# Rows of V as two half rows of 2080 bytes, and a scratch tensor with both batches side by side

## The chip, the core and the metric

The kernel runs on one core of one Trainium2 chip. The core has a matrix engine (TensorE, in the profile PE for the matmuls and PEld for its weight loads), a vector engine (DVE), a scalar engine (ACT), GpSimd (POOL) and a queue engine (SP) that here only starts transfers. Transfers between main memory (DRAM) and the on-chip memory (SBUF, 128 partitions) run on 16 DMA engines that all queues share. The metric is the device time of one execution in microseconds (us), lower is better.

## What is computed

A block-sparse attention, whose result goes through a token mixer. Cut to what matters:

```python
batch, n_heads, seq, head_dim = 4, 8, 768, 64     # 24 blocks of 32 tokens
mask = |blk_i - blk_j| <= 1, or blk_i or blk_j is 0 or 23
mask[block qb, block kb] = True for the 3 kb in sampled_blocks[qb]
attn = softmax(where(mask, q k^T / 8, -1e9));  x = attn @ v       # (4, 768, 512)

theta = x @ w_theta
y = einsum('ts,bsd->btd', w_tok_r, x * cos(theta)) + einsum(..., w_tok_i, x * sin(theta))
u = x + y
return u + maximum(u @ w_ch, 0)
```

## The kernel before

The attention works on two batches at a time (`bp` = 0, 1; in each the batches `b` = 0, 1, the pairs of head halves `e` = 0, 1). Within a pair of batches come first 8 wide units, which are the two outer blocks of queries against all keys, and then 22 ordinary units, one for each inner block `i` of 32 queries. An ordinary unit uses eight blocks of keys and values: three of the window, the three sampled ones, and the two outer ones. The work of one unit is spread over several rounds of one loop, `for n in range(len(units) + 2)`, so that different engines are on different units: scores (PE), row minimum (DVE), exponentials (ACT), transposes (PE, line 307), their copy (ACT, line 309), and the products with V (PE, line 318, `X`). The order on every engine is the order of this code; nothing is rearranged by a scheduler in the attention.

The values stand in DRAM as `vr`, one row of 1040 floats (4160 bytes) for each token and pair of batches: 2 batches x 2 x 4 heads x 65, where the 65th column is a one that makes the sum of the weights. Behind them stand 32 rows of zeros. Two tiles feed the products:

- `va` (two buffers) holds the window in partitions 0 to 95, block `k` in slot `k % 3`, and block 0 in partitions 96 to 127. Unit `i` loads two fresh blocks with `load_window` through SP: one transfer of 64 rows, or two of 32 where the slots wrap around. It is issued in the round before its use, when the unit two before has released the buffer.
- `vb` (`VB_BUFS = 3` buffers) holds the three sampled blocks in partitions 0 to 95 and block 23 in 96 to 127. `gather_v` fills it with one indirect transfer on POOL, whose row numbers stand in the table `rows`; blocks that are in the window or twice in the sample get rows of zeros. `Tables.make` works out `rows` once on DVE (lines 155 to 163).

`values` (PE) reads from both with `weigh`: 65 columns at offset `260 * (2 * b + e) + 65 * p`. `finish` scales the result and SP writes it to the scratch tensor in DRAM,

```python
xs = dram.tile([NP, 2, NB, P, P], F32, name="xs")      # pair, batch, block, row, column
```

which is two runs of 512 bytes for each of 128 rows of a unit. SP also carries the loads of `q` and of the raw weights (`raw_*`, decoded on the way by DVE and ACT); the ACT queue carries the next pair's keys (`kb`) and wide values (`vw`) once, at the change of pair. After the attention the token mix reads `xs` back (`load`, line 480, and `load_raw`, line 491), four blocks at a time in runs of 512 bytes, and is nearly all matmuls (lines 517 to 519, 555 to 557, 578 to 580).

Of the kernel before, what the change touches and what calls it, by code (L numbers as in the profile page):

```python
# [19 lines left out]
P = 128  # L20
NB = 24
NP = 2
ZEROS = float(768 * NP)
VB_BUFS = 3
# [92 lines left out]
class Tables:  # L117
# [6 lines left out]
    def make(self, nc, cp):  # L124
        raw = self.raw
        words = raw.rearrange("p (i k w) -> p i k w", k=3, w=2)
        given = cp.tile([P, 3, NB], F32, name="sb_given")
        nc.vector.tensor_copy(given, words[:, :, :, 0].rearrange("p i k -> p k i"))
        r = cp.tile([P, 3, NB], F32, name="sb_r")
        nc.vector.tensor_scalar(r, given, 0.0, float(NB - 1), op0=ALU.max, op1=ALU.min)  # L130
        self.block = cp.tile([1, NB * 3], I32, name="sb_block")
        nc.vector.tensor_copy(self.block.rearrange("p (i k) -> p k i", k=3), r[0:1])
        iota_i = cp.tile([P, NB], I32, name="iota_i")
        nc.gpsimd.iota(iota_i, pattern=[[1, NB]], base=0, channel_multiplier=0)
        qi = cp.tile([P, NB], F32, name="qi")
# [12 lines left out]
        nc.vector.scalar_tensor_tensor(t, r, float(NB - 1), r, op0=ALU.subtract, op1=ALU.mult)  # L148
        nc.vector.scalar_tensor_tensor(u, t, 0.0, u, op0=ALU.is_equal, op1=ALU.max)
        for k in range(1, 3):  # L150
            for j in range(k):
                nc.vector.tensor_tensor(t[:, j, :], r[:, k, :], r[:, j, :], op=ALU.is_equal)
                nc.vector.tensor_tensor(u[:, k, :], u[:, k, :], t[:, j, :], op=ALU.max)

        self.rows = rows = cp.tile([96, NP, NB], I32, name="rows")
        for k in range(3):
            g = slice(32 * k, 32 * k + 32)
            nc.vector.tensor_scalar(t[g, 0, :], u[g, k, :], -1.0, 1.0, op0=ALU.mult, op1=ALU.add)
            for bp in range(NP):
# [3 lines left out]
        nc.vector.tensor_scalar(rows, base, ZEROS, None, op0=ALU.add)  # L163


def attention(tc, qT, qE, kT, vr, sampled, xs, ident, pieces, follow):
# [8 lines left out]
    nc = tc.nc  # L175
    with ExitStack() as ctx, ExitStack() as early:
# [70 lines left out]
        def fresh(i, new):  # L247
# [6 lines left out]
                    runs.append([blk, 1])  # L254
            return runs

        def load_window(bp, i):
            va = vas[i % 2]
            if i <= 2:
                nc.sync.dma_start(va[96:128], vr[768 * bp : 768 * bp + 32])  # L260
            for b0, n in fresh(i, i <= 2):
                s0 = 32 * (b0 % 3)
                nc.sync.dma_start(va[s0 : s0 + 32 * n], vr[768 * bp + 32 * b0 : 768 * bp + 32 * (b0 + n)])
            st[bp, i]["va"] = va

        def gather_v(bp, i):
            vb = vbs[i % VB_BUFS]
            if i <= VB_BUFS:
                nc.sync.dma_start(vb[96:128], vr[768 * bp + 736 : 768 * bp + 768])
            nc.gpsimd.indirect_dma_start(  # L270
                out=vb[0:96],
                out_offset=None,
                in_=vr,
                in_offset=bass.IndirectOffsetOnAxis(ap=tab.rows[:, bp, i : i + 1], axis=0),
            )
            st[bp, i]["vb"] = vb

        def scores(bp, i):
# [52 lines left out]
        def values(bp, i):  # L331
            s = st[bp, i]
            s["X"] = x = ps_x.tile([P, 4, 65], F32, tag="X", name=f"X{bp}_{i}")
            for b in range(2):
                for e in range(2):
                    weigh(x, 2 * b + e, s["T"], 2 * e + b, s["va"], 96 if i == 1 else 128, 260 * (2 * b + e), True, False)
                    weigh(x, 2 * b + e, s["T"], 4 + 2 * e + b, s["vb"], 96 if i == NB - 2 else 128, 260 * (2 * b + e), False, True)
# [42 lines left out]
        def finish_wide(bp, b, e, z):  # L380
            if (e, z) == (1, 1):
                xo = normalised(f"{bp}_w{b}", xws[bp, b])
                nc.sync.dma_start(xs[bp, b, 0 : NB : NB - 1].rearrange("z r c -> r z c"), xo.rearrange("r (z e) d -> r z (e d)", z=2))
            if (b, z) == (0, 1):
                load_v_wide(bp, 1, e)

# [63 lines left out]
def token_mix(tc, w, ch_pieces, xs, outT, bias, nb):  # L450
# [8 lines left out]
    with ExitStack() as late, ExitStack() as ctx:  # L459
# [14 lines left out]
        def load(k):  # L474

            b, h, j = at(k)
            xa[k] = xp.tile([P, 4, 4, 32], F32, tag="xa", name=f"xa{k}")
            src = xs[b // 2, b % 2, 4 * j : 4 * j + 4].rearrange("i (p q) c -> p i q c", p=4)
            for p in range(4):
                nc.sync.dma_start(xa[k][:, p].rearrange("s c u -> s (c u)"), src[p])  # L480

        def load_raw(k, pool=None):
# [8 lines left out]
            nc.sync.dma_start(xr[b, j].rearrange("r i c u -> r i (c u)"), xs[b // 2, b % 2, 4 * j : 4 * j + 4].rearrange("i r c -> r i c"))  # L491

        def tok(b, j):
            return [t[:, :, 128 * (j % 3) : 128 * (j % 3) + 128] for t in xT[b, j // 3]]
# [141 lines left out]
def sparse_attention_then_token_mix(ctx, tc, qT, qE, kT, vr, sampled, w_theta, w_tok_r, w_tok_i, w_ch, outT):  # L636
# [78 lines left out]
```

## Time and profile before

| what | value |
|---|---|
| median of 3 runs | 638.6 us |
| lowest and highest run | 634.63 and 641.9 us |
| span of the profiled execution, first to last instruction | 635.0 us |
| PE, DVE, ACT, POOL busy | 563.2, 463.5, 361.0, 45.6 us |
| packets: SP queue q1, gathers q0, ACT queue q10 | 73088, 4928, 1856 |
| megabytes: q1, q0, q10 | 72.99, 17.57, 4.74 |
| share of 16 DMA engines: q1, q0, q10 | 39.2%, 10.7%, 2.1% |

Only the span is known of the profiled execution; its own device time was not recorded beside it. It stands 3.6 us below the median, inside the range of the three runs.

How to read the views. A row of a group has the line, engine and operation, what it writes and reads, its shape and count, then the busy time and the mean of one in ns, then the idle time of the engine just before and what ended it. The chain of waits goes back from the end to what released each step. A row of the DMA queues has the packets, the megabytes and the time that the packets took, as a share of 16 engines over the stretch; since packets can overlap a little, a share may pass 100%. A wait line reads: who waited, for whom, us in total, times, longest.

### The profile page before, as it was taken

Reading aid. Unit: us, or ns where it says so; the run is one execution under the profiler, and the core shown is the slowest. Engines: PE = TensorE matmul, PEld = TensorE weight load, DVE = VectorE, ACT = ScalarE, POOL = GpSimd, SP = SyncE. Lnnn points to the kernel's source line nnn. Section 1 sums busy time; section 2 is a strip of 40 time slices with the busy share of each in tenths; the row PEclk is TensorE's granted clock in tenths of the full one; section 3 lists DMA queues with packets and bytes.
Section 4 is the critical chain, followed back from the end, with each engine's and each line's share of the span. In section 5 each row is a group of like instructions: output and inputs, shape, how many; then the busy total and the mean of one; then the engine's idle time right before and its main releaser. Section 6 shows DMA issues by size and latency. Waiting matters only on the chain.

```text
span 635.0 us, 19148 instructions
## 1 busy us (share of the span) xinstructions
PE 563.2 (89%) x7808; PEld 483.1 (76%) x7808; DVE 463.5 (73%) x1239; ACT 361.0 (57%) x774; POOL 45.6 (7%) x56
## 2 busy tenths in 40 slices
PE   4987778769887768668999999999999999999997
PEld 1555545545455546547999999999999999999997
DVE  1897978875798878758999697575973767746554
ACT  1586768764587767656667564355642465524520
POOL 0101212211002211110000000000000000000000
PEclk9998989988898999887999999999999999999999
DMA  8859979999778997866542224211241211211002
GB/s 287 259 156 246 275 209 259 258 278 345 219 204 244 251 257 226 221 161 170 139 130 73 64 84 143 69 47 50 80 124 59 70 51 42 80 59 61 27 1 99
DMA packets 79959, 96.52 MB, mean 152 GB/s; under 512 B 5312, under 2 KB 64832, under 8 KB 79488
## 3 DMA queue, kind: packets, MB, share of 16 engines
q1 hardware_dynamic: 73088, 72.99, 39.2%
q0 software_dynamic: 4928, 17.57, 10.7%
q10 hardware_dynamic: 1856, 4.74, 2.1%
q8 instruction: 61, 1.00, 0.7%
q14 instruction: 26, 0.21, 0.1%
HBM read 82.70 MB, written 12.58 MB: 150 GB/s over the span
## 4 chain that ended last, share of the span: by engine, by line
PE 66%; DMA 18%; DVE 8%; issue 4%; ACT 2%; SPq 1%; DVEq 1%; ACTq 0%
PE y L555 10%; PE y L556 10%; PE y L557 10%; DMA va<-in_vr_dram 10%; PE X L318 4%; PE S L288 4%; PE T L307 4%; PE h L519 3%; PE h L518 3%; PE o L578 3%; PE h L517 3%; PE o L580 3%; PE o L579 3%; DMA kb<-in_kT_dram 3%; PE SW L357 2%
## 5 line engine op out<-in xcount | busy, mean ns | idle before, releaser
L300 ACT ACTIVATE P<-S,m 128x256 f32<-128x256 f32 x176 | 69.0, 477 | 15.1 <-DVE m L291 14.9
L307 PEld LDWEIGHTS T<-ident,P 128*128 128x128 f32 x352 | 42.1, 150 | 38.2 <-ACT P L300 25.9
L307 PE MATMUL T<-ident,P 128*128 128x128 f32 x352 | 60.5, 304 | 11.2 <-ACT P L300 6.1
L318 PE MATMUL X<-va,pT 128*32 128x65 f32 (+1 forms) x1408 | 50.3, 233 | 21.9 <-DMA va<-in_vr_dram 18.1
L291 DVE TENSOR_REDUCE m<-S 128x2 f32<-128x512 f32 x88 | 56.7, 686 | 16.7 <-PE S L288 9.8
L309 ACT COPY pT<-T 128x1024 f32<-128x1024 f32 x44 | 44.8, 1018 | 41.5 <-PE T L307 41.4
L288 PE MATMUL S<-kg,q 64*32 64x256 f32 x1408 | 55.1, 404 | 10.9 <-issue 10.9
L555 PE MATMUL y<-w_tok_r_hi,zh 128*128 128x384 f32 x192 | 64.6, 336 | 0.0
L556 PE MATMUL y<-w_tok_r_lo,zh 128*128 128x384 f32 x192 | 64.4, 335 | 0.0
L557 PE MATMUL y<-w_tok_r_hi,zl 128*128 128x384 f32 x192 | 64.3, 335 | 0.0
L556 PE MATMUL y<-w_tok_i_lo,zh 128*128 128x384 f32 x192 | 64.2, 334 | 0.0
L555 PE MATMUL y<-w_tok_i_hi,zh 128*128 128x384 f32 x192 | 64.2, 334 | 0.0
L557 PE MATMUL y<-w_tok_i_hi,zl 128*128 128x384 f32 x192 | 62.7, 334 | 0.0
L270 POOL DMA_INDIRECT vb<-in_vr_dram,rows x44 | 44.1, 1002 | 229.3 <-PE X L318 206.0
L318 PEld LDWEIGHTS X<-va,pT 128*32 128x32 f32 (+1 forms) x1408 | 35.6, 116 | 31.8 <-DMA va<-in_vr_dram 17.8
L517 PE MATMUL h<-w_theta_hi,xTh 128*128 128x256 f32 x192 | 55.8, 290 | 1.9 <-ACT xTh L508 1.9
L519 PE MATMUL h<-w_theta_hi,xTl 128*128 128x256 f32 x192 | 55.6, 290 | 0.5 <-DVE xTl L509 0.5
L518 PE MATMUL h<-w_theta_lo,xTh 128*128 128x256 f32 x192 | 55.3, 288 | 0.0
L318 PE MATMUL X<-vb,pT 128*32 128x65 f32 (+1 forms) x1408 | 49.8, 232 | 5.0 <-issue 5.0
L521 ACT ACTIVATE t<-h,up_int 128x256 f32<-128x256 f32 x48 | 22.7, 473 | 42.7 <-PE h L519 42.0
L528 ACT ACTIVATE cs<-rr 128x256 f32<-128x256 f32 x48 | 20.0, 416 | 45.8 <-DVE rr L526 45.8
L578 PE MATMUL o<-uh,w_ch_hi 128*128 128x384 f32 x128 | 42.5, 336 | 0.9 <-DVE of L584 0.9
(125 smaller groups left out, 1337.2 us busy)
## 6 DMA issues: line engine op xcount, KB each, us to landing
xa<-xs SPq DMA_DIRECT2D x192, 64.0 KB
va<-in_vr_dram SPq DMA_DIRECT2D x30, 260.0 KB
xr<-xs SPq DMA_DIRECT2D x24, 256.0 KB
out_dram<-of SPq DMA_DIRECT2D x32, 192.0 KB
q<-in_qT_dram SPq DMA_DIRECT2D x22, 256.0 KB
xs<-xo SPq DMA_DIRECT2D x44, 128.0 KB
vw<-in_vr_dram SPq DMA_DIRECT2D x6, 780.0 KB
raw_tok_r<-in_w_tok_r_dram SPq DMA_DIRECT2D x9, 512.0 KB
```

The costliest lines, as they stand in the source:

```text
L288: nc.tensor.matmul(sc[32 * p : 32 * p + 32, e, b, :], q[rows, b, p, :], kg[rows, :, 4 * b + p, :], start=True, stop=True)
L291: nc.vector.tensor_reduce(m[:, e], sc[:, e], axis=AX.X, op=ALU.min)
L300: nc.scalar.activation(pt[:, e, b, :], sc[:, e, b, :], AF.Exp, bias=m[:, e, b : b + 1], scale=-1.0)
L307: nc.tensor.transpose(t[:, k, :], pt, ident)
L318: nc.tensor.matmul(x[32 * p : 32 * p + 32, g, :], pt[0:rows, k, 32 * p : 32 * p + 32], v[0:rows, v0 + 65 * p : v0 + 65 * p + 65], start=st ...
L517: nc.tensor.matmul(ps, hi[:, c, :], wh[:, c, :], start=c == 0, stop=False)
L518: nc.tensor.matmul(ps, hi[:, c, :], wl[:, c, :], start=False, stop=False)
L519: nc.tensor.matmul(ps, lo[:, c, :], wh[:, c, :], start=False, stop=c == 3)
L555: nc.tensor.matmul(acc, zh[:, dd], wh[:, j, tt], start=j == 0 and m == 0, stop=False)
L556: nc.tensor.matmul(acc, zh[:, dd], wl[:, j, tt], start=False, stop=False)
L557: nc.tensor.matmul(acc, zl[:, dd], wh[:, j, tt], start=False, stop=j == 5 and m == 1)
L578: nc.tensor.matmul(ps, wh[:, c, :], uh, start=c == 0, stop=False)
```

## The change

Four things. The tiles `va` and `vb` become two halves of 528 floats, of which 520 are used, one half for each batch `b`; a row of `vr` lands as two runs of 2080 bytes. The loads through SP stay one transfer each, with the same rows in a three-dimensional shape. The gather becomes two indirect transfers, one for each half, over `vr` seen as half rows, with a table of row numbers of its own for each half (2 x row + h). And `xs` gets the order pair, block, row, batch, column, so that a unit's row is one run of 1024 bytes when written, and the reads of the token mix take runs of 512 bytes that are 1024 apart.

```diff
-        self.rows = rows = cp.tile([96, NP, NB], I32, name="rows")
+        self.rows = cp.tile([96, 2, NP, NB], I32, name="rows")
...
-        nc.vector.tensor_scalar(rows, base, ZEROS, None, op0=ALU.add)
+        for h in range(2):
+            nc.vector.tensor_scalar(self.rows[:, h], base, 2.0, 2.0 * ZEROS + h, op0=ALU.mult, op1=ALU.add)
...
-        vas = [cp.tile([P, 1040], F32, name=f"va{x}") for x in range(2)]
-        vbs = [cp.tile([P, 1040], F32, name=f"vb{x}") for x in range(VB_BUFS)]
+        vas = [cp.tile([P, 2, 528], F32, name=f"va{x}") for x in range(2)]
+        vbs = [cp.tile([P, 2, 528], F32, name=f"vb{x}") for x in range(VB_BUFS)]
...
+        def load_rows(t, s0, row, n):
+
+            nc.sync.dma_start(t[s0 : s0 + n, :, 0:520], vr[row : row + n].rearrange("r (h c) -> r h c", h=2))
...
-                nc.sync.dma_start(va[s0 : s0 + 32 * n], vr[768 * bp + 32 * b0 : 768 * bp + 32 * (b0 + n)])
+                load_rows(va, 32 * (b0 % 3), 768 * bp + 32 * b0, 32 * n)
...
-            nc.gpsimd.indirect_dma_start(
-                out=vb[0:96],
-                out_offset=None,
-                in_=vr,
-                in_offset=bass.IndirectOffsetOnAxis(ap=tab.rows[:, bp, i : i + 1], axis=0),
-            )
+            for h in range(2):
+                nc.gpsimd.indirect_dma_start(
+                    out=vb[0:96, h, 0:520],
+                    out_offset=None,
+                    in_=vr.rearrange("r (h c) -> (r h) c", h=2),
+                    in_offset=bass.IndirectOffsetOnAxis(ap=tab.rows[:, h, bp, i : i + 1], axis=0),
+                )
...
-                    weigh(x, 2 * b + e, s["T"], 2 * e + b, s["va"], 96 if i == 1 else 128, 260 * (2 * b + e), True, False)
+                    weigh(x, 2 * b + e, s["T"], 2 * e + b, s["va"][:, b], 96 if i == 1 else 128, 260 * e, True, False)
...
-            nc.sync.dma_start(xs[bp, :, i].rearrange("b r c -> r b c"), xo.rearrange("r (b e) d -> r b (e d)", b=2))
+            nc.sync.dma_start(xs[bp, i].rearrange("r b c -> r (b c)"), xo.rearrange("r g d -> r (g d)"))
...
-            src = xs[b // 2, b % 2, 4 * j : 4 * j + 4].rearrange("i (p q) c -> p i q c", p=4)
+            src = xs[b // 2, 4 * j : 4 * j + 4, :, b % 2].rearrange("i (p q) c -> p i q c", p=4)
...
-    xs = dram.tile([NP, 2, NB, P, P], F32, name="xs")
+    xs = dram.tile([NP, NB, P, 2, P], F32, name="xs")
```

No instruction changes places with another on any engine. On SP, in the ordinary units, the same transfers stand in the same order with other shapes. Before:

```order
36 L263 DMA va_118<-in_vr_dram 64x1040
37 L341 DMA xs<-xo_4_1107 128x2x128
38 L59 DMA raw_tok_r_1161<-in_w_tok_r_dram 128x1024
39 L263 DMA va_119<-in_vr_dram 64x1040
40 L341 DMA xs<-xo_5_1201 128x2x128
41 L203 DMA q_11_1204<-in_qT_dram 128x512
42 L263 DMA va_118<-in_vr_dram 32x1040 x2
43 L341 DMA xs<-xo_6_1297 128x2x128
```

And now, at the same place:

```order
36 L260 DMA va_118<-in_vr_dram 64x2x520
37 L346 DMA xs<-xo_4_1115 128x256
38 L59 DMA raw_tok_r_1169<-in_w_tok_r_dram 128x1024
39 L260 DMA va_119<-in_vr_dram 64x2x520
40 L346 DMA xs<-xo_5_1210 128x256
41 L204 DMA q_11_1213<-in_qT_dram 128x512
42 L260 DMA va_118<-in_vr_dram 32x2x520 x2
43 L346 DMA xs<-xo_6_1307 128x256
```

Nothing moved; the window rows have a middle dimension of 2, and the writes of `xs` have lost theirs. On POOL, from the first gathers on, each `vb` is filled by two transfers in a row where there was one. Before:

```order
15 L270 DMA vb_120<-in_vr_dram,rows 96x1040
16 L270 DMA vb_121<-in_vr_dram,rows 96x1040
17 L270 DMA vb_122<-in_vr_dram,rows 96x1040
18 L270 DMA vb_120<-in_vr_dram,rows 96x1040
19 L270 DMA vb_121<-in_vr_dram,rows 96x1040
```

And now:

```order
15 L275 DMA vb_120<-in_vr_dram,rows 96x520 x2
16 L275 DMA vb_121<-in_vr_dram,rows 96x520 x2
17 L275 DMA vb_122<-in_vr_dram,rows 96x520 x2
18 L275 DMA vb_120<-in_vr_dram,rows 96x520 x2
19 L275 DMA vb_121<-in_vr_dram,rows 96x520 x2
```

The second transfer of a pair follows the first with nothing in between.

More of the change, by code (lines that the diff above doesn't have):

```diff
@@ L259, in load_window @@
             if i <= 2:
-                nc.sync.dma_start(va[96:128], vr[768 * bp : 768 * bp + 32])
+                load_rows(va, 96, 768 * bp, 32)
             for b0, n in fresh(i, i <= 2):
-                s0 = 32 * (b0 % 3)
-                nc.sync.dma_start(va[s0 : s0 + 32 * n], vr[768 * bp + 32 * b0 : 768 * bp + 32 * (b0 + n)])
+                load_rows(va, 32 * (b0 % 3), 768 * bp + 32 * b0, 32 * n)
             st[bp, i]["va"] = va
@@ L268, in gather_v @@
             if i <= VB_BUFS:
-                nc.sync.dma_start(vb[96:128], vr[768 * bp + 736 : 768 * bp + 768])
-            nc.gpsimd.indirect_dma_start(
-                out=vb[0:96],
-                out_offset=None,
-                in_=vr,
-                in_offset=bass.IndirectOffsetOnAxis(ap=tab.rows[:, bp, i : i + 1], axis=0),
-            )
+                load_rows(vb, 96, 768 * bp + 736, 32)
+            for h in range(2):
[5 more added lines that the diff above has]
+                )
             st[bp, i]["vb"] = vb
@@ L335, in values @@
                 for e in range(2):
-                    weigh(x, 2 * b + e, s["T"], 2 * e + b, s["va"], 96 if i == 1 else 128, 260 * (2 * b + e), True, False)
-                    weigh(x, 2 * b + e, s["T"], 4 + 2 * e + b, s["vb"], 96 if i == NB - 2 else 128, 260 * (2 * b + e), False, True)
+                    weigh(x, 2 * b + e, s["T"], 2 * e + b, s["va"][:, b], 96 if i == 1 else 128, 260 * e, True, False)
+                    weigh(x, 2 * b + e, s["T"], 4 + 2 * e + b, s["vb"][:, b], 96 if i == NB - 2 else 128, 260 * e, False, True)
         def finish(bp, i):
             xo = normalised(f"{bp}_{i}", st.pop((bp, i))["X"])
-            nc.sync.dma_start(xs[bp, :, i].rearrange("b r c -> r b c"), xo.rearrange("r (b e) d -> r b (e d)", b=2))
+            nc.sync.dma_start(xs[bp, i].rearrange("r b c -> r (b c)"), xo.rearrange("r g d -> r (g d)"))
         def load_v_wide(bp, b, e, queue=nc.sync):
@@ L382, in finish_wide @@
                 xo = normalised(f"{bp}_w{b}", xws[bp, b])
-                nc.sync.dma_start(xs[bp, b, 0 : NB : NB - 1].rearrange("z r c -> r z c"), xo.rearrange("r (z e) d -> r z (e d)", z=2))
+                nc.sync.dma_start(xs[bp, 0 : NB : NB - 1, :, b].rearrange("z r c -> r z c"), xo.rearrange("r (z e) d -> r z (e d)", z=2))
             if (b, z) == (0, 1):
@@ L490, in load_raw @@
                 xr[b, j] = zp.tile([P, 4, 4, 32], F32, tag="xr", name=f"xr{b}_{j}", bufs=2)
-            nc.sync.dma_start(xr[b, j].rearrange("r i c u -> r i (c u)"), xs[b // 2, b % 2, 4 * j : 4 * j + 4].rearrange("i r c -> r i c"))
+            nc.sync.dma_start(xr[b, j].rearrange("r i c u -> r i (c u)"), xs[b // 2, 4 * j : 4 * j + 4, :, b % 2].rearrange("i r c -> r i c"))
         def tok(b, j):
```

## The prediction

> **What bounds the kernel now.** I first cut the span into three stretches, to see which engine is full in each. Columns: the stretch, its length, busy time of PE, weight load, DVE, ACT and POOL, the granted clock, the mean share of the 16 DMA engines, GB/s.
>
> ```profile
> 0.00:50.00 50.00, 39.08 (x672) 20.21 (x672) 31.84 (x86) 26.75 (x44) 4.39 (x15) 1.00 0.73 235
> 50.00:290.00 240.00, 185.82 (x5001) 126.16 (x5005) 187.64 (x482) 165.37 (x325) 41.17 (x41) 0.92 0.88 243
> 290.00:635.00 345.00, 338.32 (x2150) 336.76 (x2139) 244.04 (x671) 168.83 (x406) 0.00 (x0) 0.99 0.25 77
> ```
>
> After 290 us, the token mix, TensorE is busy for 338.32 of 345 us and the DMA engines for a quarter: a change of transfers is worth nothing there unless a load comes late. Up to 290 us, the attention, no engine is full (PE 186 and DVE 188 of 240 us), and the DMA engines are at 0.88. So the second view is the chain of waits of 50 to 290 us, by line, and beside it what PE waited for there.
>
> ```profile
> by line: DMA va<-in_vr_dram 26.3%; PE X L318 11.4%; PE S L288 10.8%; PE T L307 9.9%; issue 9.1%; DMA xr<-xs 4.4%; DMA xs<-xo 4.4%; DMA kb<-in_kT_dram 3.8%; DVE m L291 3.2%; DMA raw_tok_r<-in_w_tok_r_dram 2.7%; ACT P L300 2.4%; DVE mw L359 1
> ...
> PE X L318 <- DMA va<-in_vr_dram: 18.1, 14, 3.5
> ```
>
> The transfers make 26.3 + 4.4 + 4.4 + 3.8 + 2.7 = 41.6% of this chain. I take that share as the price of DMA-engine time: 1 us more on all 16 engines moves the end by about 0.42 us. That is an estimate: a chain picks one of several nearly equal paths. PE itself stood still for `va` 18.1 us in 14 waits, which caps what faster window loads alone can return directly. No such wait on `vb` is among PE's waits of this stretch: the gathered rows are always there in time.
>
> **What is moved, and what a packet costs now.** The third view is the DMA queues in short windows in which nearly all packets are of one size: q1 is the SP queue, q10 the ACT queue, q0 the gathers. Columns: packets, MB, share of 16 engines. In order: 400 to 500 us (512-byte rows of `xs`, mostly), 152.9 to 154.0 (1040-byte rows of `vw`), 102.5 to 103.0 (4096-byte rows of weights).
>
> ```profile
> q1 hardware_dynamic: 11614, 7.12, 23.0%
> ...
> q10 hardware_dynamic: 357, 0.39, 99.3%
> ...
> q1 hardware_dynamic: 50, 0.20, 100.2%
> ```
>
> Share times 16 engines times the window, over packets, gives 31.7 ns, 49.0 ns and 160 ns each. A line through the last two (49.0 ns at 1092 bytes on average, 160 at 4096) gives 0.037 ns a byte: 85.5 ns for 2080 bytes, and 162.4 for 4160. That line is my price for packets that nothing disturbs.
>
> **The change part by part.**
>
> *Rows of V.* Each of the 44 ordinary blocks of queries loads 64 window rows and 96 gathered rows. Each row becomes two packets of 2080 bytes: 2 x 85.5 - 162.4 = 8.6 ns more. 160 x 8.6 / 16 = 0.086 us of all engines in a block, 3.8 us in 44.
>
> *xs written as 1024-byte runs.* 256 packets of 512 bytes become 128 of 1024: 256 x 31.7 - 128 x 49.0 = 1.84 us, / 16 = 0.115 us in a block, 5.1 us in 44. The reads `xa` and `xr` keep their 512-byte packets, now 1024 bytes apart; they fall almost wholly after 290 us and I cost them at nothing. Their cover is the 0.25 above.
>
> *xs beside long rows.* At the change of batch pair, `xs` writes share the engines with the 12288-byte rows of the next `kb`. From 149.6 to 151.6 us the two queues read:
>
> ```profile
> q10 hardware_dynamic: 68, 0.80, 95.2%
> q1 hardware_dynamic: 59, 0.03, 4.8%
> ```
>
> 59 short packets between 68 long ones: an engine takes about one of each in turn, so a 512-byte packet waits for 2.0 x 16 x 0.952 / 68 = 0.45 us of a long one. The chain has that write, and DVE waited for it with its next `xo`:
>
> ```profile
> 144.07 10.50 DMA xs<-xo
> 154.67 0.42 DVE xo L328
> ...
> L328 DVE TENSOR_TENSOR xo<-X,sm 128x256 f32<-128x256 f32 x5 | 2.1, 425 | 1.8 <-DMA xs<-xo 1.6
> ```
>
> A write has 16 packets on each engine now and 8 then; 8 turns of 0.45 us are 3.6 us, more than the 1.6 us that DVE waits. So at most 1.6 us comes back; I take 1.0, since the loads of `kb` and of the weights stand behind it on the chain.
>
> The Trainium skill, in "DMA: Bandwidth & Descriptors", section "Queues, rings and completion order", has an engine drain a whole packet, typically 9 to 17 descriptors, from one queue before it turns to the next. By that rule the 16 short runs are through in one or two turns whether they are 16 or 8, this item is nothing, and the sum below is 1.0 us higher. The 59 against 68 of the trace speak for a turn after each run.
>
> *A second gather for each block.* POOL issues 88 indirect loads in place of 44, and SP as many as before. On POOL:
>
> ```profile
> L270 POOL DMA_INDIRECT vb<-in_vr_dram,rows x44 | 44.1, 1002 | 229.3 <-PE X L318 206.0 <-DVE rows L163 19.8 <-DMA vb<-in_vr_dram,rows 2.2
> ...
> 22.01 1.10 POOL L270 DMA_INDIRECT vb<-in_vr_dram,rows  x1 [19.83 <-DVE rows L163]
> 23.42 0.91 POOL L270 DMA_INDIRECT vb<-in_vr_dram,rows  x1 [0.31 <-issue]
> 24.64 0.91 POOL L270 DMA_INDIRECT vb<-in_vr_dram,rows  x1 [0.30 <-issue]
> ...
> 59.07 1.06 POOL L270 DMA_INDIRECT vb<-in_vr_dram,rows  x1 [3.14 <-PE X L318]
> ...
> 67.41 1.03 POOL L270 DMA_INDIRECT vb<-in_vr_dram,rows  x1 [4.03 <-PE X L318]
> 70.53 1.36 POOL L270 DMA_INDIRECT vb<-in_vr_dram,rows  x1 [2.09 <-PE X L318]
> ...
> 65.99 1.11 PE X L318 x64
> ...
> DMA to landing us min/median/max: 4.4/5.8/8.1
> ```
>
> Two gathers back to back start 1.2 to 1.4 us apart, so the second half of a row is asked for about 1.3 us later. POOL has 229 us to spare for 44 more us, and nothing else is queued behind. With three `vb` buffers, a buffer is used shortly before the third gather after it: 70.53 - 59.07 = 11.5 us is the shortest such step that I find. The use itself, the `X` matmuls, starts 1.4 us before the gather that it releases (65.99 against 67.41), which leaves 10.1 us. The median landing grows from 5.8 to 7.1 us, the longest from 8.1 to 9.4: just inside. Zero on the path; the cover is `VB_BUFS = 3`.
>
> What the second gather costs the DMA engines is not shown directly. The nearest row is that of the first three gathers, alone from 23.8 to 28.5 us:
>
> ```profile
> DMA packets 334, 1.17 MB, mean 249 GB/s; under 512 B 40, under 2 KB 57, under 8 KB 334
> ...
> q0 software_dynamic: 317, 1.15, 85.8%
> ```
>
> Their 288 rows took 0.858 x 16 x 4.7 / 288 = 224 ns each (some 30 small signals left out), 62 ns over 162.4; over 96 rows and 16 engines that is 0.37 us a gather. If all of it is start-up that comes once per gather, 44 more cost 16.3 us of engine time; if it overlaps with q1's packets, nothing. I take half, 8.1 us: from 50 to 290 us both queues have work most of the time.
>
> ```profile
> q1 hardware_dynamic: 26311, 36.40, 54.3%
> q0 software_dynamic: 4592, 16.38, 26.6%
> ```
>
> *Tables and PE.* DVE computes `rows` twice. One took 0.18 us, and the first gathers are not used before 53 us, while they are issued at 22: nothing. The matmuls read the same 65 columns with the same strides: nothing.
>
> ```profile
> L163 DVE TENSOR_SCALAR rows<-sb_raw x1: 184/184/184, 21.5 to 21.5; 96x48 int32<-96x48 f32 x1
> ```
>
> **The sum.** Engine time: +3.8 - 5.1 + 8.1 = +6.8 us, times 0.42 = +2.9 us on the path; the write at the change of pair -1.0. Net +1.9 us. Bounds of the same terms: (3.8 - 5.1 + 0) x 0.42 - 1.6 = -2.1, and (3.8 - 5.1 + 16.3) x 0.42 = +6.3. The profiled execution spans 635.0 us, 3.6 below the median of the runs, 638.6, which themselves lie from 634.6 to 641.9. On the median the sum gives 640.5; I say 640. About 1% is what a measurement of this kernel can tell from no change, so this is no change.
>
> **The rivals.**
>
> *A, faster: long packets suffer more from a busy system, and short ones escape it.* While a gather runs, rates fall. First 111.3 to 112.2 us, a gather almost alone; then 142 to 144 us, gather, `va` and `vw` together; the last two lines are the same windows on all engines, with the DMA share and GB/s at their end.
>
> ```profile
> q0 software_dynamic: 51, 0.21, 98.8%
> ...
> q0 software_dynamic: 63, 0.24, 54.3%
> q1 hardware_dynamic: 79, 0.10, 25.0%
> q10 hardware_dynamic: 83, 0.08, 19.1%
> ...
> 111.30:112.20 0.90, 0.90 (x62) 0.84 (x64) 0.90 (x2) 0.68 (x1) 0.00 (x0) 1.00 1.01 240
> 142.00:144.00 2.00, 0.00 (x0) 0.00 (x0) 0.00 (x0) 0.46 (x1) 0.00 (x0) 1.00 0.98 214
> ```
>
> A 4160-byte packet took 0.9 x 16 x 0.988 / 51 = 279 ns there instead of 162, and over 50 to 290 us a gathered one took 240 x 16 x 0.266 / 3938 = 259 ns (16.38 MB are 3938 rows; q0's row stands above). If every row of V fell from 259 ns to 2 x 85.5 = 171, 44 x 160 rows would give back 38.7 us of engine time, 16 on the path: 622 on the median; half of that, 630. Against it: the 1040-byte packets of q10 in the second window took 2 x 16 x 0.191 / 83 = 74 ns instead of 49, half as much again. What slows the long ones slows the short ones too, so the bytes seem to count, not the size.
>
> *B, slower: a gathered packet costs time by its number.* If what makes a gathered packet slow is its own handling (its index, its address), 2080 bytes cost what 4160 do, 259 ns: 44 x 96 x 259 / 16 = 68 us more of engine time, 28 on the path, 667. At half of it 653. It decides from 130 ns for a gathered half row, half of 259; at 159 ns the loss is 1%: 44 x 96 x (318 - 259) / 16 = 15.6 us, 6.5 on the path. For it: gathers are the slow ones even alone (224 and 279 ns). Against it: the same slow window slows other queues' packets, which have no index.
>
> **Chances.** Within 1% (632.2 to 645): 0.45, the sum and its bounds with half of A and the beginnings of B at its edges. Faster by more: 0.25, A. Slower by more: 0.30, B, with the second half of a row landing too late as its smaller part. The range leaves out the full sizes of A and of B: 626 to 656. The likeliest case's own range is 636 to 645.
>
> **What would show it.** The queue rows: q0 with about 8448 data packets and as many MB as before; q1 with 44 x 128 fewer from `xs` and some 3300 more from V. Right, if the share of q0 rises by a tenth to a quarter over 10.7% of the page, the DMA share of 50 to 290 us stays within 0.85 to 0.92, `va` keeps its place at the head of the chain, and no wait on `vb` appears. A is right if q0's share falls well below 10.7% at the same MB; B if it nears twice that. Wrong in another way, if PE or POOL begins to wait on `vb`, or the token mix, 345 us, changes its length: then the new pitch of `xs` was not free.

## The result and the profile after

| | before | after |
|---|---|---|
| median | 638.16 us (4 runs, 634.63 to 641.9) | 653.41 us (4 runs, 652.54 to 654.68) |
| span of the profiled execution | 635.0 us | 652.8 us |

The ratio is 1.0255, with a 95% interval of 1.021 to 1.030: the changed kernel is 2.5% slower. (In the tables below, ratios leave disturbed runs out and medians do not, so a ratio can differ from the quotient of two medians.)

The first question is whether the transfers became dearer. From the page of the changed kernel, the queues (packets, MB, share of 16 engines), then the stretch 50 to 290 us (length, busy times, clock, DMA share, GB/s), and its chain of waits by line:

```profile
q1 hardware_dynamic: 70720, 72.99, 37.7%
q0 software_dynamic: 5632, 17.58, 9.8%
```

```profile
50.00:290.00 240.00, 193.60 (x4835) 123.46 (x4831) 186.04 (x470) 164.27 (x322) 77.71 (x79) 0.94 0.81 232
```

```profile
by line: DMA va<-in_vr_dram 33.1%; PE S L293 14.2%; PE X L323 12.9%; PE T L312 8.9%; issue 7.5%; PE SW L362 4.0%; DVE m L296 2.7%; ACT P L305 2.5%; PE XW L323 2.3%; PE Tw L312 2.2%; SPq L59 1.3%; SPq L260 1.3%; ACT pT L314 1.1%; DVE mw L364
```

They did not. The gathers take 9.8% of the engines' time where they took 10.7%, and the DMA share of the attention fell from 0.88 to 0.81. q0 also has fewer packets than forecast. Before, 44 x 96 rows and 44 x 16 signals make its 4928 packets. After, 88 x 16 signals leave 5632 - 1408 = 4224 for the rows, as many as before, of 17.58 MB / 4224 = 4160 bytes: two half rows of one gather travel as one packet. The Trainium skill, in "DMA: Bandwidth & Descriptors", section "SWDGE vs HWDGE vs iDMA", lets a packet hold up to 64 descriptors and preferably at most 4096 bytes. The trace agrees that several runs share a packet; at 4160 bytes it goes past the size preferred there.

Where the time went is read from the starts of PE's `X` matmuls in the trace, in us. The second row is the kernel before, profiled again in run f1 below.

| kernel | to the first X | X of pair 0 | change of pair | X of pair 1 | from the last X to the end |
|---|---|---|---|---|---|
| before | 53.0 | 99.3 | 34.9 | 103.2 | 344.5 |
| before, again (f1) | 55.0 | 101.9 | 34.6 | 101.7 | 342.9 |
| after | 60.2 | 105.5 | 38.7 | 105.2 | 343.2 |

The token mix is untouched. The loss is spread over the attention, and its largest single piece lies ahead of the first `X`. There, the timeline of POOL after (start, length, idle before and what ended it):

```profile
21.88 1.11 POOL L275 DMA_INDIRECT vb<-in_vr_dram,rows  x1 [19.70 <-DVE rows L164]
23.30 0.92 POOL L275 DMA_INDIRECT vb<-in_vr_dram,rows  x1 [0.31 <-issue]
24.52 0.92 POOL L275 DMA_INDIRECT vb<-in_vr_dram,rows  x1 [0.30 <-issue]
25.75 0.92 POOL L275 DMA_INDIRECT vb<-in_vr_dram,rows  x1 [0.30 <-issue]
26.97 0.92 POOL L275 DMA_INDIRECT vb<-in_vr_dram,rows  x1 [0.30 <-issue]
28.19 0.92 POOL L275 DMA_INDIRECT vb<-in_vr_dram,rows  x1 [0.30 <-issue]
```

and in the same stretch the timelines of PE and of DVE:

```profile
23.25 1.03 PE L362 MATMUL SW<-kb,qe 64*32 64x512 f32 x12
24.21 0.88 PE L312 MATMUL Tw<-ident,PW 128*128 128x128 f32 x6
25.02 0.79 PE L323 MATMUL XW<-vw,pTw 128*32 128x65 f32 x10
26.23 0.32 PE L323 MATMUL XW<-vw,pTw 128*32 128x65 f32 x4 [0.42 <-issue]
...
29.13 0.31 PE L323 MATMUL XW<-vw,pTw 128*32 128x65 f32 x4 [1.14 <-issue]
30.56 0.74 PE L323 MATMUL XW<-vw,pTw 128*32 128x65 f32 x17 [1.12 <-issue]
```

```profile
30.67 0.96 DVE L364 TENSOR_REDUCE mw<-SW 128x1 f32<-128x768 f32 x1 [8.12 <-remote]
```

PE ended `SW` at 23.25 + 1.03 = 24.28. DVE's minimum `mw`, whose only input is `SW`, starts at 30.67, 1.56 us after the last of the six gathers ended (28.19 + 0.92 = 29.11). Meanwhile PE goes on in pieces, with nothing shown that it waits for. So PE's work was done and the others did not learn of it: the rise of PE's semaphore was held while POOL made the gathers. (A semaphore is the counter that an engine raises when a step is done and that the others wait for; the trace records each rise, and has the one that belongs to this `SW` 6.3 us after its end.) Before, with three gathers, the same minimum started 0.14 us after `SW`, at 24.32 us, in the midst of them:

```profile
24.32 0.96 DVE L359 TENSOR_REDUCE mw<-SW 128x1 f32<-128x768 f32 x1 [1.74 <-PE SW L357]
```

An ordinary block shows it in small. After, POOL, PE and DVE around 99 us:

```profile
98.86 1.03 POOL L275 DMA_INDIRECT vb<-in_vr_dram,rows  x1 [3.67 <-PE X L323]
100.56 0.92 POOL L275 DMA_INDIRECT vb<-in_vr_dram,rows  x1 [0.67 <-PE X L323]
```

```profile
98.71 0.30 PE L323 MATMUL X<-vb,pT 128*32 128x65 f32 x8
98.94 1.99 PE L293 MATMUL S<-kg,q 64*32 64x256 f32 x32
```

```profile
100.33 0.16 DVE L330 TENSOR_SCALAR sm<-X 128x4 f32<-128x4 f32 x1 [0.50 <-PE X L323]
```

`X` reads half 0 of `vb` in its first 32 matmuls, so half 0 is free in the middle of `X` and its gather starts at 98.86, before `X` ends at 99.01. DVE's `sm`, which waits for that end, starts 1.3 us later, and the gather of half 1, which waits for it too, at 100.56. PE starts 21 of the 32 matmuls of `S`, starts no other for 0.5 us, and is through in 1.99 us. Before, `S` took 1.09 us, and the gather found all of `X` done:

```profile
91.78 0.30 PE L318 MATMUL X<-vb,pT 128*32 128x65 f32 x8
92.00 1.09 PE L288 MATMUL S<-kg,q 64*32 64x256 f32 x32
```

```profile
92.38 0.91 POOL L270 DMA_INDIRECT vb<-in_vr_dram,rows  x1 [7.76 <-PE X L318]
```

Over all blocks `S` grew from 51.4 us busy to 73.8 (50 to 310 us, 43 of 44 blocks after, 41 before). My theory from here on, T: **an indirect transfer on POOL holds back the rises of PE's semaphore until about 1.4 us after its start, and 88 of them hold back more than 44.** T says two things: that there is a hold and that it belongs to the gathers, and that it is what costs the time. Rivals: the loss comes from half rows as such (packets, landing), from the halves of `va`, or from the new `xs`.

The Trainium skill, in "SBUF — State Buffer", section "SBUF: two separate sides", knows two places of contention, the port that DVE shares with GpSimd and the DMA engines' own ports, and has PE wait for nobody on its side of the memory. PE's 1.14 us without a matmul or a wait that the profile shows, while POOL gathers, is explained by neither place. Whether the hold has to do with this memory at all, no run here shows.

### The profile page after: what moved, and what is told of

It is laid out like the page before. It is cut to its first block, busy times and chain, and to the rows that moved or that the text cites. A ratio compares the mean times of both kernels' runs of the same rounds, so it can differ in the third digit from the quotient of the medians.

```text
span 652.8 us, 19232 instructions
## 1 busy us (share of the span) xinstructions
PE 581.8 (89%) x7808; PEld 488.3 (75%) x7808; DVE 465.2 (71%) x1240; ACT 363.5 (56%) x774; POOL 87.6 (13%) x100
## 3 DMA queue, kind: packets, MB, share of 16 engines
q1 hardware_dynamic: 70720, 72.99, 37.7%
q0 software_dynamic: 5632, 17.58, 9.8%
## 4 chain that ended last, share of the span: by engine, by line
PE 69%; DMA 16%; DVE 6%; issue 4%; SPq 2%; ACT 2%; DVEq 0%; ACTq 0%
DMA va<-in_vr_dram 12%; PE y L560 10%; PE y L561 10%; PE y L562 10%; PE S L293 5%; PE X L323 5%; PE SW L362 4%; PE h L524 3%; PE T L312 3%; PE o L583 3%; PE o L585 3%; PE h L523 3%; PE o L584 3%; PE h L522 3%; PE XW L323 2%
## 5 line engine op out<-in xcount | busy, mean ns | idle before, releaser
L275 POOL DMA_INDIRECT vb<-in_vr_dram,rows x88 | 86.2, 979 | 208.7 <-PE X L323 184.7
L293 PE MATMUL S<-kg,q 64*32 64x256 f32 x1408 | 74.9, 406 | 10.3 <-issue 6.5
L323 PE MATMUL X<-va,pT 128*32 128x65 f32 (+1 forms) x1408 | 48.2, 229 | 26.3 <-DMA va<-in_vr_dram 24.7
L312 PEld LDWEIGHTS T<-ident,P 128*128 128x128 f32 x352 | 40.1, 146 | 30.2 <-ACT P L305 13.7
L312 PE MATMUL T<-ident,P 128*128 128x128 f32 x352 | 54.6, 291 | 6.5 <-ACT P L305 5.4
L293 PEld LDWEIGHTS S<-kg,q 64*32 64x32 f32 x1408 | 29.6, 108 | 39.4 <-issue 25.9
L323 PE MATMUL X<-vb,pT 128*32 128x65 f32 (+1 forms) x1408 | 48.0, 228 | 3.9 <-issue 3.8
```

The source lines that it names most:

```text
L275: nc.gpsimd.indirect_dma_start(out=vb[0:96, h, 0:520], out_offset=None, in_=vr.rearrange("r (h c) -> (r h) c", h=2), in_offset=bass.Indire ...
L293: nc.tensor.matmul(sc[32 * p : 32 * p + 32, e, b, :], q[rows, b, p, :], kg[rows, :, 4 * b + p, :], start=True, stop=True)
L312: nc.tensor.transpose(t[:, k, :], pt, ident)
L323: nc.tensor.matmul(x[32 * p : 32 * p + 32, g, :], pt[0:rows, k, 32 * p : 32 * p + 32], v[0:rows, v0 + 65 * p : v0 + 65 * p + 65], start=st ...
```

## The experiments

The runs e, f, g and h were made on four chips, one letter on each, and are compared with runs of the kernel before on the same chip. Rises of PE's semaphore are counted up to 140 us: the modelled ends of the matmuls that raise it against the times at which the trace records a rise, paired in order (a few records are missing). "Late" is over 0.5 us.

```
run                           ratio to before [95%]     rises late      longest after 50 us
before (first profile)        -                         0 of 100        0.23 us
after                         1.0255 [1.0210, 1.0300]   48 of 112       1.84
e1 half 1 first               1.0392 [1.0341, 1.0444]   23 of 89        2.36
e2 xs alone                   0.9944 [0.9894, 0.9994]   14 of 100       0.93
e3 halves of va alone         1.0087 [1.0044, 1.0130]   16 of 96        0.95
e4 halves of vb alone         1.0224 [1.0169, 1.0279]   53 of 112       1.32
f1 before, again              638.0 us, one run         16 of 98        0.84
f2 first six spread           1.0179 [1.0083, 1.0276]   58 of 117       1.32
f4 a small second gather      1.0328 [1.0236, 1.0420]   21 of 88        2.44
g1 no gather                  1.0346 [1.0295, 1.0398]   0 of 87         0.08
g2 half 0 alone               0.9787 [0.9747, 0.9827]   39 of 121       1.30
g3 half 1 alone               0.9795 [0.9758, 0.9833]   16 of 102       0.88
h1 xs alone, gathers spread   1.0001 [0.9957, 1.0045]   0 of 96         0.26
h2 after, both pairs spread   1.0150 [1.0097, 1.0204]   1 of 116        0.52
```

### The parts one by one, and the order of the halves (e1 to e4)

e1 issues the gather of half 1 ahead of that of half 0, so that nothing is released in the middle of `X`; e2, e3 and e4 make one part of the change each.

```diff
-            for h in range(2):
+            for h in (1, 0):
                 nc.gpsimd.indirect_dma_start(
```

The core of e2, e3 and e4, one line each; the loads, stores, tables and offsets that go with that tile are changed as in the diff of the change:

```diff
-    xs = dram.tile([NP, 2, NB, P, P], F32, name="xs")
+    xs = dram.tile([NP, NB, P, 2, P], F32, name="xs")
```

```diff
-        vas = [cp.tile([P, 1040], F32, name=f"va{x}") for x in range(2)]
+        vas = [cp.tile([P, 2, 528], F32, name=f"va{x}") for x in range(2)]
```

```diff
-        vbs = [cp.tile([P, 1040], F32, name=f"vb{x}") for x in range(VB_BUFS)]
+        vbs = [cp.tile([P, 2, 528], F32, name=f"vb{x}") for x in range(VB_BUFS)]
```

> The changed kernel, with the gather of half 1 issued ahead of that of half 0 in each block. Half 1 is free only when X has ended, so no gather is released in the middle of X any more; 88 gathers, packets and layouts stay. Theory T (a gather that starts while X still runs holds up PE and its semaphore updates, about 0.6 us a block, and the six first gathers in a row hold up the wide units by 8 us): PE's S matmuls of 50 to 310 us fall from 74.9 us busy back to 55 to 60, the ordinary blocks come 0.4 to 0.8 us closer together, the first S stays near 46.5 us; time 636 to 645 us. Rival R (88 half-row gathers cost their time in the DMA engines, on POOL or in late landing, wherever they start): S stays near 75 us, time 650 to 656 us.

> The kernel before, with only the scratch tensor of x changed (both batches of a row side by side, 1024-byte runs written). Theory T: nothing of the loss lies here; xs writes get cheaper by 5 us of engine time and the change of pair by up to 1.6 us: 634 to 639 us. Rival (the new pitch makes the token mix's reads or the writes dearer): 645 us or more, with the token mix longer than 333 us.

> The kernel before, with only va split into two halves of 2080 bytes, loaded by one transfer as before; whole rows are still gathered. Theory T: nothing of the loss lies here; twice as many window packets of half the size, between -2 and +3 us: 636 to 642 us. Rival (window rows as shorter packets land later, PE waits longer for va): 645 us or more, PE's waits for va over 25 us in 50 to 310 us.

> The kernel before, with only vb split and gathered by two indirect transfers of half rows, half 0 first. Theory T: the whole loss and a bit more, since the lighter xs writes are missing: 652 to 658 us, S busy near 75 us, first S near 46.5 us. Rival (the loss is shared with va or xs): below 647 us.

In percent of the time before, e2 is -0.56, e3 +0.87 and e4 +2.24, together +2.55: the whole change. So the parts add up (to the digit by luck, since each has an interval of about 0.5 to either side), most of the loss is in the two gathers, and the rival of `xs` is out: that part is, if anything, a small gain. The halves of `va` cost 5.6 us, more than T allowed. PE waited for `va` 24.2 us there (50 to 310 us), less than in f1's profile (30.8). Its packets are hardly dearer: over 50 to 290 us two of 2080 bytes on q1 took 2 x 124 = 248 ns, where one of 4160 bytes took 240 and 248 in the two profiles of before. What the 5.6 us consist of stays open.

e1 missed both expectations: 664.8 us, slower than with the halves in order. Its `S` fell to 54.0 us busy as T said, but the rises were held elsewhere. POOL, PE and DVE of one block of e1:

```profile
93.31 0.92 POOL L275 DMA_INDIRECT vb<-in_vr_dram,rows  x1 [3.76 <-PE X L323]
94.54 0.92 POOL L275 DMA_INDIRECT vb<-in_vr_dram,rows  x1 [0.30 <-issue]
```

```profile
92.94 1.62 PE L293 MATMUL S<-kg,q 64*32 64x256 f32 x32
94.49 1.09 PE L312 MATMUL T<-ident,P 128*128 128x128 f32 x8
```

```profile
96.22 1.29 DVE L296 TENSOR_REDUCE m<-S 128x2 f32<-128x512 f32 x2 [1.69 <-PE T L312]
```

The two gathers now run back to back. `S` ends at 94.56, but the minimum `m` that waits for it starts at 96.22, 0.76 us after the second gather's end. A late `m` makes the exponentials late, and they the transposes `T`, for which PE waits. The profile names `T` as the releaser, since both rises came together. Over 50 to 310 us, DVE stood idle before `m` for twice as long as in the changed kernel (e1 first; the two profiles of before have 16.7 and 14.3 us, and f4 below 27.2):

```profile
L296 DVE TENSOR_REDUCE m<-S 128x2 f32<-128x512 f32 x88 | 56.7, 686 | 28.3 <-PE T L312 22.1 <-PE S L293 4.9 <-issue 1.3
```

```profile
L296 DVE TENSOR_REDUCE m<-S 128x2 f32<-128x512 f32 x88 | 56.7, 686 | 13.4 <-PE S L293 5.4 <-PE T L312 5.1 <-issue 1.3
```

So in e1 a held rise does reach the next engines; in the changed kernel it does not show at `m`. With the same bytes, transfers and layouts as the changed kernel, order alone costs 1.4%, about 9 us: the intervals of the two ratios, 1.034 to 1.044 and 1.021 to 1.030, do not meet, and on e1's own chip the parts of the changed kernel add up to the same 1.0255.

### The kernel before again, spread gathers, a small second gather (f1, f2, f4)

f2 puts a one-element copy on POOL ahead of each of the first three blocks' gathers, which reads a result of the round (first diff, in the loop over rounds); f4 adds to the kernel before a gather of 96 runs of 520 bytes behind each gather (second diff, in `gather_v`).

```diff
+                if 6 <= n <= 8:
+                    bp, i, x = units[n]
+                    s = st[(bp, i) + (x or ())]
+                    nc.gpsimd.tensor_copy(tick[:, n - 6 : n - 5], s["T"][0:1, 0, 0:1])
                 do(n + 2, gather_v)
```

```diff
+            nc.gpsimd.indirect_dma_start(
+                out=extra[i % 3][0:96],
+                out_offset=None,
+                in_=vr.rearrange("r (g c) -> (r g) c", g=8),
+                in_offset=bass.IndirectOffsetOnAxis(ap=tab.rows[:, bp, i : i + 1], axis=0),
+            )
```

> The kernel before, unchanged, profiled once more beside the runs of this study. In the profile shown of it PE's semaphore updates came on time while a gather ran (S, due 0.72 us after the gather's start, at 0.81); in the profiles of the runs e2 and e3, with the same 44 gathers, the same updates came only 1.45 us after the start. Theory T (a gather holds PE's updates until about 1.4 us after its start) expects the hold here too, time 636 to 644 us, for S is the only update that falls into it and has slack. Rival: no hold here either, so that it comes with the edits (a layout), not with the gather.

> The changed kernel, with the first three blocks' six gathers no longer issued in a row at 22 us: each pair stands behind a one-element copy on POOL that reads the turned weights of the round before, so that the pairs go out three rounds ahead of their use, as all later ones do. Theory T (six gathers in a row hold PE's updates for 6 us and the wide units with them): the first S comes at 38 to 41 us in place of 46.5, the gaps of later blocks stay, time 645 to 649 us. Rival (the wide units are slow because the gathers' transfers crowd out the loads of kb and vw): the first S gains less than 2 us, time 651 to 655 us.

> The kernel before, with a second, small gather behind each gather of V: 96 runs of 520 bytes into a scratch tile that nothing reads. It has the 88 indirect transfers of the changed kernel, in the order of run e1 (both after X), with rows of V whole, va and xs as before; 2.2 MB more are moved, 44 x 96 x 32 ns / 16 = 8 us of engine time, an estimate from the 31.7 ns of a 512-byte packet. Theory T (the number of gathers on POOL counts, not the size or place of their rows): 655 to 668 us, first S near 46.5 to 49 us, S's updates 2 us late as in e1. Rival (half rows as such are dear: their packets, their landing in two pieces): 638 to 646 us.

f1 shows the hold in the kernel before as well. One block, PE, POOL and DVE:

```profile
61.95 1.09 PE L288 MATMUL S<-kg,q 64*32 64x256 f32 x32
```

```profile
62.34 0.91 POOL L270 DMA_INDIRECT vb<-in_vr_dram,rows  x1 [4.17 <-PE X L318]
```

```profile
63.91 1.29 DVE L291 TENSOR_REDUCE m<-S 128x2 f32<-128x512 f32 x2 [0.37 <-PE S L288]
```

`S` ends at 63.04 and `m` learns of it at 63.91. So the hold does not come with the edits; the first profile, in which such rises were 0.08 us late, lacked it. It cost little there: 636.2 us of span against 635.0.

f4 came out as T had it: rows of V whole, `va` and `xs` as before, and 3.3% slower. By the expectation's own estimate, 8 us of engine time at the chain's share of 0.42, the added bytes account for about 3 of its 21 us. So a second indirect transfer costs time whatever it brings; how much of that is the hold, f4 alone does not say. DVE's first wait of the wide units is back, now with six gathers in a row, three whole and three small:

```profile
30.12 0.96 DVE L366 TENSOR_REDUCE mw<-SW 128x1 f32<-128x768 f32 x1 [7.29 <-remote]
```

f2 did its local work, and little more. The first `S` came at 41.0 us in place of 46.5 and the first `X` at 55.6 in place of 60.2, but the profiled execution ended only 1.4 us earlier than the changed kernel's, since the `X` of pair 1 took 108.9 us in place of 105.2. Its 653.1 us are what the rival expected, not T's 645 to 649, and the interval of f2's ratio holds the changed kernel's. So the 5 us ahead of the first `X`, the most striking thing in the trace, are not shown to reach the end.

### No gather, or one half (g1, g2, g3)

g1 has e2's `xs` and loads the sampled blocks, 32 rows in a row each, by three plain transfers on SP, with the first rows read from a table. g2 and g3 gather one half only (8.79 MB fewer, by their q0 rows). The diffs are of g1, in place of the gather, and of g2; g3 has h = 1.

```diff
+            _, starts = nc.values_load_multi_w_load_instructions(
+                tab.start[0:1, bp, 3 * i : 3 * i + 3], engines=[mybir.EngineType.SP], min_val=0, max_val=int(ZEROS),
+                skip_runtime_bounds_check_because="Tables clamps the block numbers",
+            )
+            for k, start in enumerate(starts):
+                nc.sync.dma_start(vb[32 * k : 32 * k + 32], vr[bass.ds(start, 32)])
```

```diff
-            for h in range(2):
+            for h in (0,):
                 nc.gpsimd.indirect_dma_start(
```

> The kernel before with the new scratch tensor of x, and without any gather: the three sampled blocks of a unit are 32 rows in a row each, so SP reads their three first rows from a table of its own and loads them as three plain transfers of 32 whole rows. POOL issues no transfer. Theory T (indirect transfers on POOL hold PE's updates): no update of PE comes more than 0.3 us late, the first S comes at 37 to 39 us, time 628 to 638 us if SP keeps up. Rival (the transfers' number on SP's queue, a table read and three more transfers a block, holds up va and xs behind them): the holds vanish but PE waits longer for va, 640 us or more.

> The changed kernel, gathering only half 0 of each sampled row: half 1 is left out, its tile is set to zero once. 44 gathers of 96 half rows, each released in the middle of X, 8.2 MB fewer moved than in the changed kernel. Theory T (what counts is which of PE's updates fall into the 1.4 us after a gather's start): X's two last updates are 1.0 to 1.3 us late in most blocks and S's on time; slower than half 1 alone by 3 to 12 us. Rival (the place of the start is of no account): equal to half 1 alone within 2 us.

> The changed kernel, gathering only half 1 of each sampled row (half 0 is left out, its tile set to zero once). 44 gathers of 96 half rows, each released by X's end as in the kernel before. Theory T: X's updates on time, S's about 0.7 us late, as in the kernel before; first S at 38 to 41 us; with 8.2 MB fewer to move 630 to 640 us. Rival (a half row costs what a whole row does, or the loss is in the halves of va): 645 us or more.

Without gathers none of 87 rises is late, in the prologue or later: the hold belongs to them. The kernel is slower for the rival's reason. PE waits longer for `va` than in any other run, as SP has a table read and three more transfers ahead of it (f1 first, then g1, 50 to 310 us):

```profile
PE X L318 <- DMA va<-in_vr_dram: 30.8, 16, 4.1
```

```profile
PE X L332 <- DMA va<-in_vr_dram: 37.1, 18, 4.9
```

g2 and g3 refute a part of T. The one holds 38 rises of `X`, most for 1.2 to 1.3 us, the other 14 of `S` for 0.7 to 0.9, with the same 8.79 MB gathered, and their times are equal. The matmuls of `S`, stretched by the hold of `X` in g2 as in the changed kernel (73.8 us), cost g2 nothing against g3 (41 blocks each, 50 to 310 us):

```profile
L295 PE MATMUL S<-kg,q 64*32 64x256 f32 x1312 | 71.9, 397 | 4.5 <-issue 0.6 <-ACT pTw L316 0.5
```

```profile
L295 PE MATMUL S<-kg,q 64*32 64x256 f32 x1312 | 50.0, 407 | 2.7 <-issue 1.5 <-ACT pTw L316 0.7 <-ACT pT L316 0.5
```

So it makes no difference where a single hold falls, and nothing here shows that a single one costs time at all. g3's 625.5 us also lie below the 630 to 640 expected. Together with the parts they split the loss in another way. e2 and e3 add up to +0.3%; halving the gathered bytes takes that to -2.05% (g3), so 8.79 MB are worth about 2.4%, 15 us. Their 2112 packets at 259 ns are 34 us of all engines, so 0.44 us of the end for each: the chain's 0.42. Adding the second half costs 4.6% (g3 to after): those 2.4% for the bytes, and 2.2% for the second transfer. That 2.2% is no second measurement beside e4's: g3 drops out of the difference, and it is the whole change less e2 and e3. (Numbers of different chips stand side by side here.)

### Gathers spread at both pairs (h1, h2)

```diff
-                if 6 <= n <= 8:
+                if n in (6, 7, 8, 36, 37, 38):
```

> The kernel before with the new scratch tensor of x alone (as run e2: 0.994 of before), and with the first three gathers of each pair of batches spread over three rounds, each behind a one-element copy on POOL as in run f2. Theory T (gathers in a row hold PE's updates until 1.7 us after the last one's start): the wide units lose their hold of 1.6 us before the first S, and 1 to 2 us at the change of pair; 632 to 637 us, the fastest correct kernel of this study. Rival (the hold there is made up later by transfers that bound the attention, as run f2 hints): as e2, 636 to 640 us.

> The changed kernel with the first three blocks' gathers of both pairs of batches spread over three rounds, as run f2 did for the first pair alone. Theory T: the 5 us before the first X and the 4 us at the change of pair both come back, what stays is the two gathers of every block: 643 to 648 us. Rival (time won by then is given back to the transfers that bound the blocks after it, as in f2, which won 4.6 us to its first X and 0.3 at the end): 650 to 654 us.

h2 came out as T had it, 1.0% better than the changed kernel, but its profile says that this need not be due to the edit. The ordinary blocks, which the edit does not touch, have no hold either. PE, POOL and DVE of one of them:

```profile
93.62 0.30 PE L324 MATMUL X<-vb,pT 128*32 128x65 f32 x8
93.85 1.09 PE L294 MATMUL S<-kg,q 64*32 64x256 f32 x32
```

```profile
93.77 1.03 POOL L276 DMA_INDIRECT vb<-in_vr_dram,rows  x1 [4.12 <-PE X L324]
95.11 0.92 POOL L276 DMA_INDIRECT vb<-in_vr_dram,rows  x1 [0.30 <-issue]
```

The gather starts in the middle of `X` as at 98.86 us of the changed kernel, but `S` takes 1.09 us. In h1 and h2, which ran on one chip, and in the first profile of before, rises are hardly held; in all profiles of gathering kernels on the other three chips of the study, and in that of the changed kernel, they are. f2 has the same copies at the first pair and the full hold. So the length of the hold goes with the chip or the execution, not with the kernel, and spreading and chip can't be told apart in h2: the changed kernel wasn't run on that chip.

h2 also limits what the hold can account for. With 1 late rise of 116 it is still 1.5% (0.97 to 2.04) slower than the kernel before on its chip, so more than half of the 2.55% is there almost without holds, as far as chips compare. Its profiled execution is 11.3 us shorter than the changed kernel's, 3.7 of them ahead of the first `X` and 7.2 at the change of pair, where the gathers no longer stand in a row. The `X` of the two pairs take 211.3 us together, for 210.7 in the changed kernel and 202.5 and 203.6 in the two profiles of before: there the hold is gone and the loss is not (one execution each). e3, with halves of `va` and whole gathers, has 214.2, e4 207.3. f2 has the hold and a ratio of 1.0179, which can't be told from h2's 1.0150. What lengthens the ordinary blocks stays open; the halves of `va` would fit e3 and h2, and no run here tests that further.

h1 gained nothing over before; no version here that computes the whole result beats the kernel before by more than e2's 0.56%.

## Why the prediction was right in its range and wrong in its reason

The time, 653.4 us, lies within the 626 to 656 us stated, but by luck: that end of the range stood for half of rival B, which did not happen. The likeliest case, no change with 636 to 645 us, was wrong, and the case that held, slower, held for another reason than the one given.

- **What bounds the kernel**: right. `va` heads the chain, at 33.1%, and no wait on `vb` appears. The price of engine time, 0.42 us of the end for each, came out at 0.44 from g3, uncertain by about a third.
- **A second gather for each block**: the step that failed. It said: "POOL has 229 us to spare for 44 more us, and nothing else is queued behind", and put only the DMA engines' start-up into the sum, 8.1 us of engine time, 3.4 on the path. Measured alone (e4) it costs 14.3 us, with less engine time, not more (q0 10.0% for 10.7%). The cover named, `VB_BUFS = 3`, held. So the cost is not in the gathers' engine time, where the prediction looked for it. What it left out is what PE's finished work waits for while POOL is busy: with 88 transfers, two in a block and six in a row at each pair's beginning, rises of PE's semaphore come up to 1.8 us late in the blocks and 6.3 us where six stand in a row. In the profile at hand this could not be read, for it is one in which the hold was 0.2 us at most. That the holds are what costs the 14.3 us is not shown: in e1 and f4 they reach DVE's `m`, but g2 with 38 of them and g3 with 14 take the same time, and h2 loses 1.5% with hardly any. So that the second transfer costs time is shown, and why it does stays open.
- **Rows of V**: mis-sized, and half of its mechanism did not happen. 44 x 64 window rows at 8.6 ns were to cost 1.5 us of engine time, 0.6 on the path; e3 measured 0.87%, 5.6 us (2.8 to 8.3). Two half rows took at most 8 ns more than a whole one there, as forecast, so the loss is not in engine time. The gathered half rows did not become more packets at all.
- **xs**: right in size: -5.1 x 0.42 - 1.0 = -3.1 us forecast, -3.6 us measured in e2 (-6.8 to -0.4). Whether the last 1.0 us, the write beside `kb`, exists can't be said: `xo` waited for `xs` 0.2 us in f1 between 140 and 180 us and not at all in e2, where the first profile had 1.6.
- **Tables, PE, token mix**: right. DVE's two `rows` are not in the way, and the token mix kept its length, 343.2 us.
- **Rival A**: fell; e3 makes short packets of long ones and is slower. **Rival B**: its half price, 653 us, equals the measured time by chance. It rested on dear packets, and q0's share fell. f4 has whole rows and is slower still.
- **What would show it**: the share of q0 was to rise and fell; 8448 data packets were forecast and 4224 came; q1's packets came as forecast (73088 - 44 x 128 + some 3300; 70720 came); the DMA share of 0.85 to 0.92 was 0.81, in part since the same megabytes had more time (232 GB/s for 243).

## What to carry to other kernels

An engine with idle time is not free to take more transfers: ask what the other engines can't do while it works, and look in the trace at an engine's end against the start of what waits for it, above all where the profile names "issue" or "remote". Cost an indirect transfer per instruction as well as per byte, and don't split one in two for the layout's sake. A stall that one profile does not show may come in the next, so take the profile twice before a step is costed at nothing. A striking gap in the trace is worth only what its removal brings at the end, and a version that keeps most of the loss without the gap, as h2 here, says that the gap is not the whole cause.

## What the runs showed of the hardware

Indirect transfers on POOL hold the rises of PE's semaphore: most of those due in the first 0.8 us of one come 1.3 to 1.5 us after its start, with two back to back 1.6 to 1.9 us after the second's start, with six in a row up to 6.3 us late. Where the rise of `X` is held, PE starts about 20 matmuls more and then none for a while (21 in the block shown). Without gathers (g1) none of 87 rises was late. The hold was there in ten profiles of gathering kernels, on at least three chips, and no rise was more than 0.52 us late in three others (before, h1, h2). Why it differs, by which path POOL reaches PE's semaphore, and how much of the lost time the hold accounts for, is open. Rows of 2080 bytes that one gather brings travel two to a packet of 4160 bytes (88 gathers, 4224 data packets).
